# An adaLN attention + FFN layer on one core: a rebuilt prologue (load order, paired tiles, projections one group further ahead, gates on VectorE, early flag)

## Chip, cores, metric

One core of a Trainium2 chip. The metric is the device time of one execution in microseconds, the median of several. The profile's span is some 2 us shorter than the time of the same run. A run is called fast, unless it is more than 1.5% above the fastest run of the same kernel (slow); comparisons below are between fast runs where there are enough of them. "Cold" below means that TensorE runs at half of its clock, as the profile's granted clock shows it (0.50); up to a trace's first recorded change it shows 1.00 even where matmuls take twice as long (380 ns from 24.37 to 28.45 in the profile before, 190 from there).

## The reference

A transformer layer with adaptive layer norm, 2048 tokens of width 448, bf16. Attention is local: a query sees 8 keys, 2 apart, at or before its own position.

```python
mod = (silu(c) @ w_mod).reshape(1, 6, 1, 448)       # sa, ca, ga, sb, cb, gb
h = layernorm(x) * (1 + ca) + sa
x = x + ga * attention(h, wqkv, wo)                  # 16 heads of 28, window 8, dilation 2
h = layernorm(x) * (1 + cb) + sb
x = x + gb * (silu(h @ w1) @ w2)                     # 448 -> 1792 -> 448
```

## The kernel before

Tokens are split by parity, 8 tiles of 128 for each. Six groups (three for each parity) go through: projection to q, k, v; logits of blocks of 114 queries against 128 keys; exponential; multiplication by a band mask; attention output; output projection and residual; second norm; FFN. The order of instructions on each engine is the order in which the Python emits them. `weave` mixes two lists of units by their estimated cost. The gates `ga` and `gb` are multiplied into `wo` and `w2` once.

```python
    def modulate(ps, n, dst, c0, which):             # (x - mean) * rstd, transposed in PSUM -> h1T or h2T
        for k in range(KT):
            V.tensor_scalar(out=dst[:, k, c0:c0 + n], in0=ps[0:KP, k, 0:n], scalar1=..., scalar2=..., op0=ALU.mult, op1=ALU.add)

    def mod_cols(vecs, dst0):                        # modulation vectors as columns
        for i, v in enumerate(vecs):
            for j in range(KT):
                for k in range(KT):
                    T.matmul(ps[:, i, j:j + 1], lhsT=wmod[:, k, v * D + KP * j:v * D + KP * j + 128], rhs=scT[:, k:k + 1], ...)
    ...
    ps0 = transposes(normalize([0, 1, 2, 3], ...))
    mod_cols((0, 1), 0)
    modulate(ps0, 512, h1T[0], HALO, 0)
    for kk in range(KT):                             # q/k weights padded from 28 to 32 columns a head
        V.tensor_copy(out=wp[:, kk, :, 0:DH], in_=wqkv[:, kk, 0:2 * D]...)
    run(project(0))
    ln1([4, 5, 6, 7])
    mod_cols((3, 4), 2); gate(0, 2); gate(1, 5)
    G.tensor_tensor(out=wo[:], in0=wo[:], in1=gbc[0:KP, 0, :]..., op=ALU.mult)
    for f in range(NF):
        G.tensor_tensor(out=w2[:, f, :], in0=w2[:, f, :], in1=gbc[:, 1, :], op=ALU.mult)

    for k in range(NG):
        fill = []
        if k >= 1: fill += ln2_units(k - 1)          # normalise, then transposes + modulate
        if k in (0, 1): fill += project(k + 1)
        if k >= 2: fill += f2_units(k - 2)
        run(weave(l_units(k), fill))
        main = f1_units(k - 1) if k >= 1 else []
        if 2 <= k < NG - 1: main = weave(main[:-2], project(k + 1)) + main[-2:]
        if k == 0: main = [ln1 of tiles 8-11, ln1 of tiles 12-15]
        run(weave(main, o_units(k) + [ln2_stats(k)]))
    run(weave(f2_units(NG - 2), ln2_units(NG - 1))); run(f1_units(NG - 1)); run(f2_units(NG - 1))
    # here: are all softmax sums in range? count, matmul, flag, values_load -> If(bad): run a safe version
```

Of the kernel before, what the change touches and what calls it, by code (L numbers as in the profile page):

```python
# [15 lines left out]
D = 448  # L16
# [50 lines left out]
def layer(ctx, tc, io, safe):  # L67
# [17 lines left out]
    cT = ct([KP, KT], "cT")  # L85
# [13 lines left out]
    nc.scalar.dma_start(out=cT[:], in_=c.rearrange("o (k p) -> p (o k)", p=KP))  # L99
    xload(0, 4)  # L100
    nc.sync.dma_start(out=wmod[:, :, 0:2 * D], in_=rows(w_mod[:, 0:2 * D]))
    nc.sync.dma_start(out=wqkv[:, 0:2, :], in_=rows(A_wqkv)[:, 0:2, :])
    nc.sync.dma_start(out=wqkv[:, 2:4, :], in_=rows(A_wqkv)[:, 2:4, :])
    xload(4, 8)
    nc.sync.dma_start(out=wmod[:, :, 2 * D:6 * D], in_=rows(w_mod[:, 2 * D:6 * D]))
    nc.sync.dma_start(out=wo[:], in_=rows(A_wo))
# [10 lines left out]
    NV, NP, NX = 8, 5, 6  # L117
# [68 lines left out]
    def transposes(ts):  # L186
        ps = big.tile([128, KT, 512], BF16, name="ps_t", tag="big")
        for j, t in enumerate(ts):
            for k in range(KT):
                T.transpose(ps[:, k, 128 * j:128 * j + 128], t[:, KP * k:KP * k + 128], ident[:])  # L190
        return ps

    def modulate(ps, n, dst, c0, which):

        for k in range(KT):
            V.tensor_scalar(out=dst[:, k, c0:c0 + n], in0=ps[0:KP, k, 0:n], scalar1=modc[:, 2 * which + 1, k:k + 1],  # L196
                            scalar2=modc[:, 2 * which, k:k + 1], op0=ALU.mult, op1=ALU.add)

    def mod_cols(vecs, dst0):

        ps = one.tile([128, 2, KT], F32, name="ps_m", tag="one")
        for i, v in enumerate(vecs):
            for j in range(KT):
                for k in range(KT):
                    T.matmul(ps[:, i, j:j + 1], lhsT=wmod[:, k, v * D + KP * j:v * D + KP * j + 128], rhs=scT[:, k:k + 1],
                             start=(k == 0), stop=(k == KT - 1))
# [101 lines left out]
    def o_units(k):  # L308
# [34 lines left out]
        units = []  # L343
        done = list(tiles)
        for i, b in enumerate(blocks):
            units.append((500.0, lambda b=b: av(b)))
            if i:
                units.append((250.0, lambda b=blocks[i - 1]: tr(b)))
            while done and i and 128 * (done[0] + 1) <= BQ * blocks[i - 1] + nq_of(blocks[i - 1]):
                units.append((750.0, lambda a=done.pop(0): wo_unit(a)))  # L350
        units.append((250.0, lambda b=blocks[-1]: tr(b)))
        for a in done:
            units.append((750.0, lambda a=a: wo_unit(a)))
# [12 lines left out]
    def ln2_units(k):  # L366
# [5 lines left out]
        def tr():  # L372
            ps = transposes(ln2[k])
            modulate(ps, 128 * len(us), h2T[k % 2], 0, 1)
# [35 lines left out]


    def ln1(us):
        mv, rs = stats(us)
        ps = transposes(normalize(us, mv, rs))
        modulate(ps, 128 * len(us), h1T[us[0] // 8], HALO + 128 * (us[0] % 8), 0)

    mv0, rs0 = stats([0, 1, 2, 3])
    S.activation(out=scT[:], in_=cT[:], func=ACTF.Silu)
    xn0 = normalize([0, 1, 2, 3], mv0, rs0)
    ps0 = transposes(xn0)  # L420
    mod_cols((0, 1), 0)
    modulate(ps0, 512, h1T[0], HALO, 0)
# [4 lines left out]
    run(project(0))  # L427
    ln1([4, 5, 6, 7])
    mod_cols((3, 4), 2)
    gate(0, 2)  # L430
    gate(1, 5)

    def gates_apply():
        G.tensor_tensor(out=wo[:], in0=wo[:], in1=gbc[0:KP, 0, :].unsqueeze(1).to_broadcast([KP, KT, D]), op=ALU.mult)
        for f in range(NF):
            G.tensor_tensor(out=w2[:, f, :], in0=w2[:, f, :], in1=gbc[:, 1, :], op=ALU.mult)  # L436

    gates_apply()

    NG = len(GROUPS)  # L440
    for k in range(NG):
        fill = []
        if k >= 1:
            fill += ln2_units(k - 1)
        if k in (0, 1):
            fill += project(k + 1)
        if k >= 2:
# [81 lines left out]
```

## Time and profile before

| | before |
|---|---|
| time, median of 3 | 276.86 us (275.07 to 279.4) |
| span of the profiled run | 271.9 us |
| TensorE busy, mean granted clock | 201.5 us, 0.885 |
| VectorE, ScalarE, GpSimd busy | 134.3, 96.1, 34.1 us |
| first q/k matmul | 24.4 us |
| first logits of group 0 / of group 1 | 45.0 / 99.4 us |
| first FFN matmul / first of the second FFN product | 113.1 / 131.0 us |
| last output row / end of the span | 264.4 / 271.9 us |

The table is read as stages: the times are when TensorE first does the named work, and the difference of two is the length of a stage. The lines of the profile stand in the prediction.

### The profile page before, as it was taken

How to read it: one execution, taken by the hardware profiler on the slowest of the kernel's cores; microseconds unless marked ns; L12 is line 12 of the kernel's file. 1: busy time of each engine (PE TensorE's matmuls, PEld its weight loads, DVE VectorE, ACT ScalarE, POOL GpSimd, SP SyncE). 2: the span in 40 equal slices, each digit the busy share in tenths (PEclk: the TensorE clock that was granted, in tenths of full speed). 3: DMA queues.
4: the chain of work that ended last, by engine and by line, in shares of the span. 5: the costliest groups of instructions: out<-in, count | busy, mean ns of one | idle time of the engine just before them, and what ended most of it. 6: DMA issues, size and time to landing. Idle time of an engine off the chain costs nothing.

```text
span 271.9 us, 4115 instructions
## 1 busy us (share of the span) xinstructions
PE 201.5 (74%) x1738; PEld 119.6 (44%) x1738; DVE 134.3 (49%) x277; ACT 96.1 (35%) x122; POOL 34.1 (13%) x66
## 2 busy tenths in 40 slices
PE   0304959808157246979999999998999999899980
PEld 0301444403053215645455554575657654555830
DVE  1505362695574664555643616656656544543020
ACT  2000224612200012843553268731883373540500
POOL 1510016990100101000000010000100010010000
PEclk9999985656855556999999999999999999999996
DMA  5999920000000000000010000000000001000000
GB/s 139 261 281 295 292 68 1 2 0 0 0 0 2 0 0 0 2 0 2 0 54 0 0 2 17 23 14 2 0 19 17 2 0 36 17 0 29 24 17 28
DMA packets 9048, 11.22 MB, mean 41 GB/s; under 512 B 896, under 2 KB 7680, under 8 KB 9024
## 3 DMA queue, kind: packets, MB, share of 16 engines
q1 hardware_dynamic: 8560, 10.90, 14.5%
q8 instruction: 15, 0.25, 0.4%
q10 hardware_dynamic: 464, 0.00, 0.1%
q14 instruction: 9, 0.07, 0.1%
HBM read 9.06 MB, written 1.84 MB: 40 GB/s over the span
## 4 chain that ended last, share of the span: by engine, by line
PE 62%; DVE 20%; DMA 7%; ACT 3%; issue 2%; POOL 2%; SPq 1%; ACTq 0%; POOLq 0%
PE ps_y L401 16%; PE ps_h L385 14%; PE ps_qk L225 12%; DMA wmod<-in_w_mod_dram 7%; PE ps_wo L340 6%; DVE p L292 5%; PE ps_v L233 4%; PE ps_t L190 4%; DVE st L171 4%; PE ps_l L255 3%; DVE h1T L196 2%; DVE o L325 2%; ACT p L257 2%; POOL rs L174 2%; PE ps_o L320 2%
## 5 line engine op out<-in xcount | busy, mean ns | idle before, releaser
L385 PE MATMUL ps_h<-h2T,w 112*128 112x384 bf16 (+1 forms) x336 | 53.1, 308 | 0.0
L257 ACT ACTIVATE p<-ps_l 128x912 bf16<-128x912 f32 (+1 forms) x36 | 33.0, 932 | 52.3 <-PE ps_l L255 52.2
L386 ACT ACTIVATE hid<-ps_h 128x768 bf16<-128x768 f32 (+1 forms) x42 | 31.0, 740 | 48.5 <-PE ps_h L385 48.5
L401 PE MATMUL ps_y<-w,hid 128*128 128x448 bf16 x224 | 46.6, 353 | 0.0
L225 PE MATMUL ps_qk<-h1T,wp 112*128 112x456 bf16 (+2 forms) x192 | 37.8, 351 | 11.2 <-DVE qk L227 8.3
L292 DVE TENSOR_TENSOR p<-p,maskb 128x1824 bf16<-128x1824 bf16 (+1 forms) x18 | 30.1, 1673 | 28.2 <-ACT p L257 28.1
L385 PEld LDWEIGHTS <-w 112*128 112x128 bf16 x336 | 32.3, 98 | 16.4
L190 PE MATMUL ps_t<-ident,xn 128*128 128x128 bf16 x128 | 13.0, 274 | 30.5 <-DVE xn L182 30.5
L225 PEld LDWEIGHTS <-wp 112*128 112x128 bf16 x192 | 19.7, 108 | 23.9 <-issue 10.9
L401 PEld LDWEIGHTS <-hid 128*128 128x128 bf16 x224 | 20.2, 98 | 17.7
L173 POOL TENSOR_TENSOR rs<-mv,epsb 128x4 f32<-128x4 f32 (+2 forms) x10 | 2.0, 197 | 200.8 <-DVE mv L172 200.8
L190 PEld LDWEIGHTS <-xn 128*128 128x128 bf16 x128 | 10.5, 124 | 33.5 <-DVE xn L182 32.6
L340 PE MATMUL ps_wo<-wo,oT 112*128 112x448 bf16 x64 | 17.1, 396 | 8.3 <-DVE oT L334 8.3
L171 DVE BATCH_NORM_STATS2 st<-x_all 128x6 f32<-128x448 bf16 x32 | 19.3, 602 | 4.9 <-DMA x_all<-in_A_x_dram 4.9
L227 ACT CAST qk<-ps_qk 128x912 bf16<-128x912 f32 (+2 forms) x12 | 8.7, 729 | 35.6 <-PE ps_qk L225 35.5
L341 DVE TENSOR_TENSOR x_all<-ps_wo,x_all 128x448 bf16<-128x448 f32 x16 | 10.0, 625 | 19.3 <-PE ps_wo L340 19.3
L405 DVE TENSOR_TENSOR ot<-ps_y,x_all 128x448 bf16<-128x448 f32 x16 | 9.9, 621 | 18.1 <-PE ps_y L401 18.1
L182 DVE TENSOR_SCALAR xn<-x_all,mv,rs 128x448 bf16<-128x448 bf16 x32 | 11.1, 404 | 12.8 <-POOL rs L174 12.8
L227 DVE CAST qk<-ps_qk 128x912 bf16<-128x912 f32 (+2 forms) x12 | 10.4, 866 | 12.1 <-PE ps_qk L225 11.9
L233 PE MATMUL ps_v<-wqkv,h1T 112*128 112x448 bf16 x72 | 15.8, 363 | 0.7 <-ACT v L235 0.7
L196 DVE TENSOR_SCALAR h2T<-ps_t,modc 112x384 bf16<-112x384 bf16 (+1 forms) x24 | 9.3, 449 | 11.2 <-PE ps_t L190 11.2
L436 POOL TENSOR_TENSOR w<-w,gbc 128x448 bf16<-128x448 bf16 x14 | 14.8, 1100 | 0.0
(58 smaller groups left out, 157.9 us busy)
## 6 DMA issues: line engine op xcount, KB each, us to landing
w<-in_B_w_dram SPq DMA_DIRECT2D x2, 1568.0 KB, 19.0
x_all<-in_A_x_dram SPq DMA_DIRECT2D x4, 448.0 KB, 14.1
out_dram<-ot SPq DMA_DIRECT2D x16, 112.0 KB, 1.7
wmod<-in_w_mod_dram SPq DMA_DIRECT2D x1, 1568.0 KB, 17.7
wqkv<-in_A_wqkv_dram SPq DMA_DIRECT2D x2, 588.0 KB, 10.7
wmod<-in_w_mod_dram SPq DMA_DIRECT2D x1, 784.0 KB, 8.1
wo<-in_A_wo_dram SPq DMA_DIRECT2D x1, 392.0 KB, 18.3
cT<-in_c_dram ACTq DMA_DIRECT2D x1, 0.9 KB, 5.5
```

What stands on the lines that cost most here:

```text
L171: V.bn_stats(out=st[:, j, :], in_=x_all[:, u, :])
L190: T.transpose(ps[:, k, 128 * j:128 * j + 128], t[:, KP * k:KP * k + 128], ident[:])
L225: T.matmul(ps[:, j, 0:n], lhsT=wp[:, k, 16 * typ + 4 * g:16 * typ + 4 * g + 4, :].rearrange("p h d -> p (h d)"), rhs=h1T[par][:, k, HALO + ...
L227: (S.copy if on_act else V.tensor_copy)(out=dst, in_=ps[:, :, 0:n])
L233: T.matmul(ps[:, j, 0:D], lhsT=h1T[par][:, k, BQ * b + 2:BQ * b + 130], rhs=wqkv[:, k, 2 * D:3 * D], start=(k == 0), stop=(k == KT - 1))
L257: S.activation(out=pbuf(par, b)[:, t, :, :, 0:nq], in_=ps[:, :, 0:4 * nq].rearrange("p j (g q) -> p j g q", q=nq), func=ACTF.Exp, scale=SCALE)
L292: V.tensor_tensor(out=p, in0=p, in1=maskb[:, 1 if b == 0 else 0, 0:nq].unsqueeze(1).to_broadcast([128, H, nq]), op=ALU.mult)
L340: T.matmul(ps[:, 0:D], lhsT=oT[par][:, kk, 128 * a:128 * a + 128], rhs=wo[:, kk, :], start=(kk == 0), stop=(kk == KT - 1))
L385: T.matmul(ps[:, j, 0:n], lhsT=w1[:, kk, 128 * f:128 * f + 128], rhs=h2T[k % 2][:, kk, 0:n], start=(kk == 0), stop=(kk == KT - 1))
L386: S.activation(out=hid[k % 2][:, 2 * i:2 * i + 2, 0:n], in_=ps[:, :, 0:n], func=ACTF.Silu)
L401: T.matmul(ps[:, 0:D], lhsT=hid[k % 2][:, f, 128 * j:128 * j + 128], rhs=w2[:, f, :], start=(f == 0), stop=(f == NF - 1))
L436: G.tensor_tensor(out=w2[:, f, :], in0=w2[:, f, :], in1=gbc[:, 1, :], op=ALU.mult)
```

## The change

Its intent: get TensorE going earlier, and keep it fed until the dense part.

```diff
-    nc.sync.dma_start(out=wqkv[:, 0:2, :], ...)           # q, k and v columns together
+    xload(0, 2); xload(2, 4)                              # was xload(0, 4)
+    nc.sync.dma_start(out=wqkv[:, 0:2, 0:2 * D], ...)     # q and k first, v later; wo before the rest of w_mod
@@ mod_cols
+                    m = 128 if j < KT - 1 else KP
-                    T.matmul(ps[:, i, j:j + 1], lhsT=wmod[:, k, v*D + KP*j : v*D + KP*j + 128], ...)
+                    T.matmul(ps[0:m, i, j:j + 1], lhsT=wmod[:, k, v*D + KP*j : v*D + KP*j + m], ...)
@@ modulate
+            if k in act: S.activation(out=o, in_=i, func=ACTF.Identity, scale=scale, bias=shift)    # act=(1, 3) in the first norm
@@ gates
-        G.tensor_tensor(wo) and 14 x G.tensor_tensor(w2[:, f, :])
+        V.tensor_tensor(wo)                               # with late_mod, at the end of group 0's logits
+        V.tensor_tensor(w2[:, f0:f1, :])                  # (0, 7) and (7, 14), at the end of group 1's logits
@@ main order
-    run(project(0)); ln1([4, 5, 6, 7])
+    run(weave(project(0), ln1_units([4, 5, 6, 7])))
     for k in range(NG):
+        if k == 0:   fill = project(1) + [late_mod]
+        elif k == 1: fill = ln2_units(0) + project(3) + [gate_w2(0, 7), gate_w2(7, 14)]
+        else:
+            f2 = f2_units(k - 2)
+            fill = f2[:2] + ln2_units(k - 1) + f2[2:]     # was ln2_units first
+        main for k == 0: project(2) + ln1 of 8-11 + ln1 of 12-15;  for 2 <= k < NG - 2: project(k + 2) with f1
+    # output projections one block later; ln2_stats ahead of the last two f1 units
+    bad = check_sums()                                    # before the last second product, was at the very end
```

(Cut: the conditioning vector `c` is loaded in rows and transposed by a small matmul instead of a strided load, ten v buffers instead of eight, the first two logits units of group 1 ahead of its `fill`, helper signatures.)

More of the change, by code (lines that the diff above doesn't have):

```diff
@@ L84, in layer @@
     x_all = ct([128, 16, D], "x_all")
-    cT = ct([KP, KT], "cT")
+    c4 = ct([KT, KP], "c4")
+    sc4 = ct([KT, KP], "sc4")
     wmod = ct([KP, KT, 6 * D], "wmod")
@@ L97, in xload @@
         nc.sync.dma_start(out=x_all[:, u0:u1, :], in_=x_view[u0 // 8, u0 % 8:u0 % 8 + u1 - u0].rearrange("a p d -> p a d"))
-    nc.scalar.dma_start(out=cT[:], in_=c.rearrange("o (k p) -> p (o k)", p=KP))
-    xload(0, 4)
+    nc.scalar.dma_start(out=c4[:], in_=c.rearrange("o (k p) -> (o k) p", p=KP))
+    xload(0, 2)
+    xload(2, 4)
     nc.sync.dma_start(out=wmod[:, :, 0:2 * D], in_=rows(w_mod[:, 0:2 * D]))
-    nc.sync.dma_start(out=wqkv[:, 0:2, :], in_=rows(A_wqkv)[:, 0:2, :])
-    nc.sync.dma_start(out=wqkv[:, 2:4, :], in_=rows(A_wqkv)[:, 2:4, :])
+    nc.sync.dma_start(out=wqkv[:, 0:2, 0:2 * D], in_=rows(A_wqkv[:, 0:2 * D])[:, 0:2, :])
+    nc.sync.dma_start(out=wqkv[:, 2:4, 0:2 * D], in_=rows(A_wqkv[:, 0:2 * D])[:, 2:4, :])
     xload(4, 8)
+    nc.sync.dma_start(out=wqkv[:, :, 2 * D:3 * D], in_=rows(A_wqkv[:, 2 * D:3 * D]))
+    nc.sync.dma_start(out=wo[:], in_=rows(A_wo))
     nc.sync.dma_start(out=wmod[:, :, 2 * D:6 * D], in_=rows(w_mod[:, 2 * D:6 * D]))
-    nc.sync.dma_start(out=wo[:], in_=rows(A_wo))
     xload(8, 12)
@@ L116, in layer @@
     hid = [ct([128, NF, 384], f"hid{i}") for i in range(2)]
-    NV, NP, NX = 8, 5, 6
+    NV, NP, NX = 10, 5, 6
     vb = [ct([128, H, 32], f"v{i}") for i in range(NV)]
@@ L184, in normalize, with transposes, modulate @@
         return got
-    def transposes(ts):
-        ps = big.tile([128, KT, 512], BF16, name="ps_t", tag="big")
+    def transposes(ts, ps=None, j0=0):
+        if ps is None:
+            ps = big.tile([128, KT, 512], BF16, name="ps_t", tag="big")
         for j, t in enumerate(ts):
+            c0 = 128 * (j0 + j)
             for k in range(KT):
-                T.transpose(ps[:, k, 128 * j:128 * j + 128], t[:, KP * k:KP * k + 128], ident[:])
+                T.transpose(ps[:, k, c0:c0 + 128], t[:, KP * k:KP * k + 128], ident[:])
         return ps
-    def modulate(ps, n, dst, c0, which):
+    def modulate(ps, p0, n, dst, c0, which, act=()):
         for k in range(KT):
-            V.tensor_scalar(out=dst[:, k, c0:c0 + n], in0=ps[0:KP, k, 0:n], scalar1=modc[:, 2 * which + 1, k:k + 1],
-                            scalar2=modc[:, 2 * which, k:k + 1], op0=ALU.mult, op1=ALU.add)
+            o, i = dst[:, k, c0:c0 + n], ps[0:KP, k, p0:p0 + n]
+            scale, shift = modc[:, 2 * which + 1, k:k + 1], modc[:, 2 * which, k:k + 1]
+            if k in act:
+                S.activation(out=o, in_=i, func=ACTF.Identity, scale=scale, bias=shift)
+            else:
+                V.tensor_scalar(out=o, in0=i, scalar1=scale, scalar2=shift, op0=ALU.mult, op1=ALU.add)
     def mod_cols(vecs, dst0):
@@ L204, in mod_cols @@
                 for k in range(KT):
-                    T.matmul(ps[:, i, j:j + 1], lhsT=wmod[:, k, v * D + KP * j:v * D + KP * j + 128], rhs=scT[:, k:k + 1],
+                    m = 128 if j < KT - 1 else KP
+                    T.matmul(ps[0:m, i, j:j + 1], lhsT=wmod[:, k, v * D + KP * j:v * D + KP * j + m], rhs=scT[:, k:k + 1],
                              start=(k == 0), stop=(k == KT - 1))
@@ L341, in wo_unit @@
             V.tensor_tensor(out=x_all[:, u, :], in0=ps[:, 0:D], in1=x_all[:, u, :], op=ALU.add)
-        units = []
-        done = list(tiles)
-        for i, b in enumerate(blocks):
-            units.append((500.0, lambda b=b: av(b)))
-            if i:
-                units.append((250.0, lambda b=blocks[i - 1]: tr(b)))
-            while done and i and 128 * (done[0] + 1) <= BQ * blocks[i - 1] + nq_of(blocks[i - 1]):
-                units.append((750.0, lambda a=done.pop(0): wo_unit(a)))
-        units.append((250.0, lambda b=blocks[-1]: tr(b)))
-        for a in done:
-            units.append((750.0, lambda a=a: wo_unit(a)))
+        units, waiting, done = [], list(tiles), 0
+        for i in range(len(blocks) + 2):
+            if i < len(blocks):
+                units.append((500.0, lambda b=blocks[i]: av(b)))
+            if 1 <= i <= len(blocks):
+                units.append((250.0, lambda b=blocks[i - 1]: tr(b)))
+            if i >= 2:
+                done = BQ * blocks[i - 2] + nq_of(blocks[i - 2])
+                while waiting and 128 * (waiting[0] + 1) <= done:
+                    units.append((750.0, lambda a=waiting.pop(0): wo_unit(a)))
         return units
@@ L373, in tr @@
             ps = transposes(ln2[k])
-            modulate(ps, 128 * len(us), h2T[k % 2], 0, 1)
+            modulate(ps, 0, 128 * len(us), h2T[k % 2], 0, 1)
         return [(10.0, norm), (700.0, tr)]
@@ L409, in f2_units, with check_sums @@
         return units
-    def ln1(us):
-        mv, rs = stats(us)
-        ps = transposes(normalize(us, mv, rs))
-        modulate(ps, 128 * len(us), h1T[us[0] // 8], HALO + 128 * (us[0] % 8), 0)
-    mv0, rs0 = stats([0, 1, 2, 3])
-    S.activation(out=scT[:], in_=cT[:], func=ACTF.Silu)
-    xn0 = normalize([0, 1, 2, 3], mv0, rs0)
-    ps0 = transposes(xn0)
+    def check_sums():
+        n = 2 * NB * H
+        ok = small.tile([128, n], F32, name="ok", bufs=1)
+        cnt = small.tile([128, 1], F32, name="cnt", bufs=1)
+        flag = small.tile([1, 1], I32, name="flag", bufs=1)
+        rcf = rc[:].rearrange("p b h -> p (b h)")
+        V.tensor_scalar(out=ok[:], in0=rcf, scalar1=LO, scalar2=None, op0=ALU.is_ge)
+        V.scalar_tensor_tensor(out=ok[:], in0=rcf, scalar=HI, in1=ok[:], op0=ALU.is_le, op1=ALU.mult)
+        V.tensor_reduce(out=cnt[:], in_=ok[:], axis=AX.X, op=ALU.add)
+        ps = one.tile([128, 512], F32, name="ps_f", tag="one")
+        T.matmul(ps[0:1, 0:1], lhsT=cnt[:], rhs=onesf[:], start=True, stop=True)
+        V.tensor_scalar(out=flag[:], in0=ps[0:1, 0:1], scalar1=-1.0, scalar2=float(128 * n), op0=ALU.mult, op1=ALU.add)
+        return nc.values_load(flag[:], min_val=0, max_val=128 * n)
@@ new lines, in ln1_units, with st, norm, tr @@
+    def ln1_units(us):
+        held = {}
+        def st():
+            held["s"] = stats(us)
+        def norm():
+            mv, rs = held["s"]
+            held["x"] = []
+            for j, u in enumerate(us):
+                t = xn[xc[0] % NX]
+                xc[0] += 1
+                V.tensor_scalar(out=t[:, 0:D], in0=x_all[:, u, :], scalar1=mv[:, j, 0:1], scalar2=rs[:, j:j + 1], op0=ALU.subtract, op1=ALU.mult)
+                held["x"].append(t)
+        def tr():
+            ps = transposes(held["x"])
+            modulate(ps, 0, 128 * len(us), h1T[us[0] // 8], HALO + 128 * (us[0] % 8), 0, act=(1, 3))
+        return [(10.0, st), (10.0, norm), (900.0, tr)]
@@ L421, in layer @@
+    st0 = stats([0, 1])
+    st1 = stats([2, 3])
+    S.activation(out=sc4[:], in_=c4[:], func=ACTF.Silu)
+    ps_c = one.tile([128, 512], F32, name="ps_c", tag="one")
+    T.matmul(ps_c[0:KP, 0:KT], lhsT=sc4[:], rhs=ident[0:KT, 0:KT], start=True, stop=True)
+    S.copy(out=scT[:], in_=ps_c[0:KP, 0:KT])
+    xa = normalize([0, 1], *st0)
+    ps0 = transposes(xa)
+    xb = normalize([2, 3], *st1)
     mod_cols((0, 1), 0)
-    modulate(ps0, 512, h1T[0], HALO, 0)
+    ps1 = transposes(xb)
+    modulate(ps0, 0, 256, h1T[0], HALO, 0, act=(1, 3))
@@ L423, in layer @@
+    modulate(ps1, 0, 256, h1T[0], HALO + 256, 0, act=(1, 3))
     for kk in range(KT):
@@ L426, in layer @@
     V.tensor_copy(out=screp[:], in_=scT[:].unsqueeze(2).to_broadcast([KP, KT, 128]))
-    run(project(0))
-    ln1([4, 5, 6, 7])
-    mod_cols((3, 4), 2)
-    gate(0, 2)
-    gate(1, 5)
-    def gates_apply():
-        G.tensor_tensor(out=wo[:], in0=wo[:], in1=gbc[0:KP, 0, :].unsqueeze(1).to_broadcast([KP, KT, D]), op=ALU.mult)
-        for f in range(NF):
-            G.tensor_tensor(out=w2[:, f, :], in0=w2[:, f, :], in1=gbc[:, 1, :], op=ALU.mult)
-    gates_apply()
+    run(weave(project(0), ln1_units([4, 5, 6, 7])))
@@ L440, in layer, with late_mod, gate_w2 @@
+    def late_mod():
+        mod_cols((3, 4), 2)
+        gate(0, 2)
+        gate(1, 5)
+        V.tensor_tensor(out=wo[:], in0=wo[:], in1=gbc[0:KP, 0, :].unsqueeze(1).to_broadcast([KP, KT, D]), op=ALU.mult)
+    def gate_w2(f0, f1):
+        V.tensor_tensor(out=w2[:, f0:f1, :], in0=w2[:, f0:f1, :], in1=gbc[:, 1, :].unsqueeze(1).to_broadcast([128, f1 - f0, D]), op=ALU.mult)
     NG = len(GROUPS)
     for k in range(NG):
-        fill = []
-        if k >= 1:
-            fill += ln2_units(k - 1)
@@ L445, in layer @@
-        if k in (0, 1):
-            fill += project(k + 1)
-        if k >= 2:
-            fill += f2_units(k - 2)
-        run(weave(l_units(k), fill))
-        main = []
-        if k >= 1:
-            main = f1_units(k - 1)
-        if 2 <= k < NG - 1:
-            main = weave(main[:-2], project(k + 1)) + main[-2:]
-        if k == 0:
-            main = [(1000.0, lambda: ln1([8, 9, 10, 11])), (1000.0, lambda: ln1([12, 13, 14, 15]))]
-        run(weave(main, o_units(k) + [(2500.0, lambda k=k: ln2_stats(k))]))
+        if k == 0:
+            fill = project(1) + [(2000.0, late_mod)]
+        elif k == 1:
+            fill = ln2_units(0) + project(3) + [(10.0, lambda: gate_w2(0, 7)), (10.0, lambda: gate_w2(7, 14))]
+        else:
+            f2 = f2_units(k - 2)
+            fill = f2[:2] + ln2_units(k - 1) + f2[2:]
@@ new lines, in layer @@
+        lu = l_units(k)
+        n0 = 2 if k == 1 else 0
+        run(lu[:n0] + weave(lu[n0:], fill))
+        if k == 0:
+            main = project(2) + ln1_units([8, 9, 10, 11]) + ln1_units([12, 13, 14, 15])
+        else:
+            main = f1_units(k - 1)
+            if 2 <= k < NG - 2:
+                main = weave(main[:-2], project(k + 2)) + main[-2:]
+        run(weave(main[:-2], o_units(k)) + [(0.0, lambda k=k: ln2_stats(k))] + main[-2:])
+    if not safe:
+        bad = check_sums()
@@ L460, in layer @@
     run(f2_units(NG - 1))
-    if safe:
-        return None
-    ok = small.tile([128, 2 * NB * H], F32, name="ok", bufs=1)
-    cnt = small.tile([128, 1], F32, name="cnt", bufs=1)
-    flag = small.tile([1, 1], I32, name="flag", bufs=1)
-    rcf = rc[:].rearrange("p b h -> p (b h)")
-    V.tensor_scalar(out=ok[:], in0=rcf, scalar1=LO, scalar2=None, op0=ALU.is_ge)
-    V.scalar_tensor_tensor(out=ok[:], in0=rcf, scalar=HI, in1=ok[:], op0=ALU.is_le, op1=ALU.mult)
-    V.tensor_reduce(out=cnt[:], in_=ok[:], axis=AX.X, op=ALU.add)
-    ps = one.tile([128, 512], F32, name="ps_f", tag="one")
-    T.matmul(ps[0:1, 0:1], lhsT=cnt[:], rhs=onesf[:], start=True, stop=True)
-    V.tensor_scalar(out=flag[:], in0=ps[0:1, 0:1], scalar1=-1.0, scalar2=float(128 * 2 * NB * H), op0=ALU.mult, op1=ALU.add)
-    return nc.values_load(flag[:], min_val=0, max_val=128 * 2 * NB * H)
+    return None if safe else bad
 @with_exitstack
```

## The prediction

> **What bounds the kernel now.** I read the slices of the page first (busy tenths, 6.8 us each), then the timeline of the first 130 us, then sums by stretch, then the end of the chain of waits.
>
> ```profile
> PE   0304959808157246979999999998999999899980
> ...
> POOL 1510016990100101000000010000100010010000
> PEclk9999985656855556999999999999999999999996
> ...
> GB/s 139 261 281 295 292 68 1 2 0 0 0 0 2 0 0 0 2 0 2 0 54 0 0 2 17 23 14 2 0 19 17 2 0 36 17 0 29 24 17 28
> ```
>
> From slice 17 on (113 us) TensorE is busy at 90% or more at full clock: it is the bound there. Before that it is idle or at about half clock. The slices read as two kernels: a ragged prologue of some 110 us and a dense part of some 150 us. By stretch (columns: span, then busy us and count of PE, PEld, DVE, ACT, POOL, then granted clock):
>
> ```profile
> 53.50:61.60 8.10, 0.00 (x0) 0.00 (x0) 8.10 (x3) 1.69 (x2) 8.10 (x8) 0.63 0.01 2
> ...
> 131.00:163.00 32.00, 31.51 (x239) 17.25 (x237) 13.57 (x25) 15.04 (x19) 0.89 (x2) 1.00 0.04 12
> 163.00:194.00 31.00, 29.34 (x296) 18.21 (x295) 18.58 (x37) 16.33 (x22) 1.04 (x2) 1.00 0.04 12
> ```
>
> The timeline (start, us, engine, line, what; in brackets the idle time before it and what ended it) says why the prologue is slow, in three places. The first three lines are TensorE's alone:
>
> ```profile
> 12.87 0.93 PE L205 MATMUL ps_m<-scT,wmod 112*128 112x1 bf16 x28
> 21.54 0.26 PE L205 MATMUL ps_m<-scT,wmod 112*128 112x1 bf16 x4 [7.74 <-DMA wmod<-in_w_mod_dram]
> 24.37 8.29 PE L225 MATMUL ps_qk<-h1T,wp 112*128 112x456 bf16 x32 [2.56 <-DVE wp L424]
> ...
> 47.00 14.76 POOL L436 TENSOR_TENSOR w<-w,gbc 128x448 bf16<-128x448 bf16 x14
> ...
> 49.63 11.24 DVE L292 TENSOR_TENSOR p<-p,maskb 128x1824 bf16<-128x1824 bf16 x1 [7.07 <-ACT p L257]
> ...
> 74.00 1.01 POOL L174 TENSOR_TENSOR rs<-rs,negh 128x4 f32<-128x4 f32 x1
> 75.04 1.31 DVE L182 TENSOR_SCALAR xn<-x_all,mv,rs 128x448 bf16<-128x448 bf16 x4 [1.40 <-POOL rs L174]
> ```
>
> First, 28 of the 32 modulation matmuls run at 12.9 us, the last four only at 21.5, after a load. They are the last column block of the second vector: columns 784 to 912 of w_mod, 16 columns past the first load's 896, so they wait for the second w_mod load, though its 16 columns are never used. Second, the mask multiply at 49.63 takes 11.24 us, against a median of 1.11 us, while GpSimd gates w2. Third, from 70 to 104 us VectorE runs norm statistics and attention output in one queue, itself waiting 1.40 us for GpSimd's power step in each round, and TensorE waits behind it.
>
> [...] the 456-column matmuls from 24.37 go at 380 ns until 28.45, then at 190. [...]
>
> **The change, part by part.**
>
> *Start.* The last block of each vector is now 112 columns wide, so the false wait goes. q and k weights load before v weights. Landing times of the old loads fit "bytes ahead of it divided by the GB/s row, plus 1.5 us". With 0.459 MB of tokens, 0.803 of w_mod and 0.803 of q/k weights ahead, that gives 9.6 us for w_mod, 12.6 for q/k, and 14.3 for the next four token tiles (2.52 MB). Chain: first pair of tiles lands at about 5.2; four statistics at 0.73 end at 8.2; normalised 8.95 and 10.15; 32 matmuls at about 0.033 end near 11; the second pair's transposes near 12; modulation in halves over VectorE and ScalarE until 12.8; first weight copy 0.32. First q/k matmul at about 13.1 against 24.4: **-11.3**.
>
> *First projections with tiles 4 to 7.* The build order puts their transposes after only 8 of the 32 q/k matmuls. Those end at 16.2 (8 x 0.38, cold). Statistics cannot start before 14.3: 2.9, GpSimd 1.3, the first normalise 0.4, so TensorE idles until 19.2. Then transposes 1.9, 24 q/k matmuls (3.0 cold, 1.6, 1.6), 16 v matmuls 3.2: first logits near 30.7, against 45.0. Cumulative **-14.3**; the new wait at 16 eats part of the overlap.
>
> *Logits of group 0.* GpSimd gates no more. VectorE does it: wo 1.1 us, w2 in two operations of 1.9 (rate of the mask, 1824 elements in 1.11 us). ScalarE now paces: 8 exponentials 7.5, table load 1.3, two q/k copies 1.5, three v copies 1.5, two gate copies 1.1, plus the first matmuls and the last mask: about 15.3 against 24.6 (45.0 to 69.6). It ends at 46. Cumulative **-24**.
>
> *Tiles 8 to 15 with attention output of group 0.* VectorE has 8+3 statistics at 0.73, 8 normalises at 0.33, four modulations at 0.54 (the other four go to ScalarE), four attention blocks (0.87+0.39), three residual adds at 0.62, two q/k copies at 0.63: 21.0 us. Statistics are still behind attention in its order, each round holds a GpSimd step of 1.3 us, and TensorE sits between them at half clock, so I add about 8 us of waits: 46 to 75, against 69.6 to 99.4. Cumulative **-24.5**. This stage also takes in group 2's projection.
>
> *Logits of group 1.* This holds group 3's projection (32 matmuls at 190 and 16 at 190 ns warm, 9.2 us), the second layer norm and the w2 gating: about 18 us, starting cold, against 13.7. Cumulative **-20**. The first FFN stays at 16 to 17.
>
> *Dense part.* The 9.2 us of group 3's projection is gone from it and TensorE bounds it, so all of that counts: **-29**. FFN matmuls ahead of the transposes, and output projections one block later, fill waits: TensorE idles only about 3.4 us of 131 to 264 (133 less the 129.6 busy in the stretches), so I give 2: **-31**.
>
> *End.* The old end, from the chain of waits:
>
> ```profile
> 263.80 0.62 DVE ot L405
> 264.42 0.23 DVE ok L469
> ...
> 265.90 0.15 DVE flag L474
> ```
>
> The check takes 1.6 us behind the last output, then 5.85 us pass to the span's end (271.9) with the flag's register load, the branch and the barrier. Now the flag is read before the last FFN. [...] At the end remain an output store (1.7 us to landing), branch and barrier. About 4 saved[...]: **-34** as the rounded sum.
>
> 276.9 - 34 is 243; I put **242 us**.
>
> **Rivals.**
>
> 1. *The start moves and the prologue stretches by as much*, because VectorE's queue from 70 to 100 us is the real bound. For it: 19.7 us of VectorE work there do not shrink much and gating adds 4.9. Against: the 11.2 us mask stall is real idle time on TensorE (0.00 busy in 53.5 to 61.6), and projections now fill gaps. It would keep only the mask and the dense part's gain: about 255.
>
> 2. *TensorE falls to half clock from 20 to 90 us.* The group-0 logits then cost TensorE about 23 us, not 15, and group 1's projection 6 more: about 254. The clock row (5 and 6 in most of the prologue) speaks for it; work packed more densely after 20 us speaks against.
>
> 3. *It goes better*: half of the 8 us of waits do not come and everything is warm after 25 us. Then 232 or so; TensorE's 201.5 us of busy time, inflated by cold matmuls, would allow even less.
>
> 4. *Loads land later*, since q/k rows are shorter (1792 bytes, not 2688). Tiles and w_mod rows are that short already and ran at 260 to 295 GB/s, so I expect under 2 us.
>
> **Range and chances.** The -11.3, the mask and the dense part rest on single lines and together are over 28 us. What is uncertain is how the two prologue stages fill: 12 us either way. Range 230 to 256. To stay within 2% (271.3) nearly all of it would have to come back. Faster 0.97, same 0.02, slower 0.01.
>
> **What would show each step.** The 32 modulation matmuls in one run near 10 to 11 us; first q/k matmul at 12 to 14.5; a TensorE gap of about 3 us before tiles 4 to 7 are transposed; every mask multiply at about 1.1 us, GpSimd busy below 20 us in all; logits of group 0 over by 44 to 50; first FFN matmul at 88 to 98; from its end to the last output about 11 us less than 131 to 264; [...] under 4 us after the last output. I am wrong if the first q/k matmul stays past 16 us, if the gating on VectorE holds up attention output by more than its 4.9 us, or if the dense stages show new waits for ScalarE.

Passages are cut out of it where the text is marked: rules and figures that no trace or run of this case shows. That GpSimd's gating makes the mask slow thus rests on the two lines of the trace alone, the one mask of 11.24 us beside 14.76 us of gating, against a median of 1.11 us; it was the author's reading until the gating was moved alone, below. Terms are cut from the sum: its parts came to -34 us with a term for TensorE's stall at the flag, which took a little over 1 us back and whose size no trace showed. The terms left add up to -35; the figure stays 242 us.

## The result

| | before | after | after / before |
|---|---|---|---|
| time, median of 4 | 277.1 us (275.07 to 279.4) | 245.38 us (243.57 to 251.07) | 0.8855 (0.8753 to 0.8957) |
| span of the profiled run | 271.9 | 244.5 | |

The ratio is the mean time of one kernel's fast runs over that of the other's of the same rounds, so not quite the ratio of the medians. The output is correct. The three fast runs after are 246.31, 244.46 and 243.57 us, at granted clocks of 0.929, 0.949 and 0.950; the profile is that of the first.

Stages, in us. "Predicted" is what the working of the prediction gives for the same points.

| TensorE first does | before | predicted | after |
|---|---|---|---|
| q/k matmul | 24.4 | 13.1 | 15.3 |
| logits, group 0 | 45.0 | 30.7 | 31.8 |
| logits, group 1 | 99.4 | 75 | 73.7 |
| FFN | 113.1 | 93 | 92.6 |
| second FFN product | 131.0 | 109.5 | 108.9 |
| (dense part, to the last output row) | 133.4 long | 11 less | 131.4 long |
| (from there to the end of the span) | 7.5 long | 4 less | 4.2 long |

First the slices of the page after the change (6.1 us each):

```profile
PE   0555979982522997899999959899599999989992
...
POOL 3801000001030000010000100000100010010000
PEclk9998999998555699999999988999889999999999
```

GpSimd's long 9s are gone, TensorE is dense from slice 13 (80 us) instead of 17 (113 us). But in the dense part there are two new 5s, with the clock at 8 around them. They were not there before. The timeline of the prologue after the change shows the modulation matmuls in one run, and the masks without the long wait:

```profile
10.10 1.55 PE L215 MATMUL ps_m<-scT,wmod 112*128 112x1 bf16 x32 [2.01 <-DMA wmod<-in_w_mod_dram]
...
15.32 3.22 PE L235 MATMUL ps_qk<-h1T,wp 112*128 112x456 bf16 x8 [2.80 <-DVE wp L471]
...
36.58 1.11 DVE L302 TENSOR_TENSOR p<-p,maskb 128x1824 bf16<-128x1824 bf16 x1 [6.62 <-ACT p L267]
```

The dense part by stretch, before and after (span, then busy us and count of TensorE, weight loads, VectorE, ScalarE, GpSimd, then clock):

```profile
131.04:264.42 133.38, 129.38 (x1108) 77.45 (x1104) 63.82 (x127) 63.83 (x80) 3.88 (x8) 1.00 0.04 14
```

```profile
108.91:240.34 131.43, 123.63 (x1074) 75.36 (x1070) 64.03 (x132) 61.41 (x75) 5.10 (x10) 0.97 0.05 14
```

TensorE's idle time there grew from 4.0 to 7.8 us, and its busy time fell by 5.75 us only, though the 9.2 us of group 3's projection were gone. The rest, about 3.5 us, is what cold matmuls took longer (clock 0.97 instead of 1.00). The clock is at half twice there (columns: span, then TensorE's busy us and count, clock, DMA):

```profile
144.91:148.32 3.41, 3.41 (x17) 0.50 0.10 34
175.62:179.03 3.41, 3.41 (x24) 0.50 0.02 5
```

The timeline at the first of the two 5s, VectorE and TensorE:

```profile
141.61 1.11 DVE L302 TENSOR_TENSOR p<-p,maskb 128x1824 bf16<-128x1824 bf16 x1 [6.46 <-ACT p L267]
142.64 0.70 DVE L185 TENSOR_SCALAR xn<-x_all,mv,rs 128x448 bf16<-128x448 bf16 x2
...
143.09 0.70 PE L195 MATMUL ps_t<-ident,xn 128*128 128x128 bf16 x8 [2.81 <-DVE xn L185]
```

TensorE waits 2.81 us for the normalised rows (`xn`) of the second norm. The normalise itself waits for nothing but its place: it stands behind the first mask multiply in VectorE's queue, and the mask waits for two exponentials, which wait for ScalarE's switch of function tables (`ACT_TABLE_LOAD`, 1.28 us) behind the last SiLUs. At 175.57 it happens again, 2.60 us. This is what `f2[:2]` ahead of the norm did. In stages with three or four blocks of logits, `weave` emits the second logits unit, which ends with the mask, before it gets past the two FFN pieces to the normalise. In stages 2 and 5, with two blocks, the normalise comes first and there is no gap.

At the end, the flag and the last output row:

```profile
219.01 0.15 DVE L433 TENSOR_SCALAR flag<-ps_f 1x1 int32<-1x1 f32 x1 [0.74 <-PE ps_f L432]
219.71 1.11 PE L411 MATMUL ps_y<-w,hid 128*128 128x448 bf16 x5 [0.74 <-DVE flag L433]
...
239.72 0.62 DVE L415 TENSOR_TENSOR ot<-ps_y,x_all 128x448 bf16<-128x448 f32 x1 [2.02 <-PE ps_y L411]
```

TensorE pays 0.74 us in the middle. 4.2 us remain after the last row (240.34 to 244.5), against 7.5.

### The profile page after: what moved, and what is told of

The parts are those of the page before. It is cut to its first block, busy times and chain, and to the rows that moved or that the text cites. A ratio compares the mean times of both kernels' runs of the same rounds, so it can differ in the third digit from the quotient of the medians.

```text
span 244.5 us, 4117 instructions
## 1 busy us (share of the span) xinstructions
PE 196.3 (80%) x1739; PEld 118.7 (49%) x1739; DVE 125.3 (51%) x274; ACT 102.9 (42%) x133; POOL 16.8 (7%) x55
## 4 chain that ended last, share of the span: by engine, by line
PE 67%; DVE 15%; ACT 8%; DMA 3%; issue 3%; POOL 1%; SPq 0%; ACTq 0%
PE ps_h L395 18%; PE ps_y L411 17%; PE ps_qk L235 10%; PE ps_v L243 5%; PE ps_wo L350 5%; PE ps_t L195 4%; ACT p L267 4%; DMA wmod<-in_w_mod_dram 3%; PE ps_l L265 3%; DVE st L174 3%; DVE p L302 2%; DVE o L335 2%; PE ps_o L330 2%; ACT h1T L204 2%; ACT L267 2%
## 5 line engine op out<-in xcount | busy, mean ns | idle before, releaser
L411 PE MATMUL ps_y<-w,hid 128*128 128x448 bf16 x224 | 48.5, 365 | 0.7 <-DVE flag L433 0.7
L302 DVE TENSOR_TENSOR p<-p,maskb 128x1824 bf16<-128x1824 bf16 (+1 forms) x18 | 19.9, 1107 | 37.5 <-ACT p L267 37.5
L235 PE MATMUL ps_qk<-h1T,wp 112*128 112x456 bf16 (+2 forms) x192 | 35.3, 334 | 4.2 <-DVE wp L471 2.8
L195 PE MATMUL ps_t<-ident,xn 128*128 128x128 bf16 x128 | 13.3, 276 | 26.4 <-DVE xn L449 14.7
L235 PEld LDWEIGHTS <-wp 112*128 112x128 bf16 x192 | 18.6, 103 | 15.6 <-issue 5.2
L174 DVE BATCH_NORM_STATS2 st<-x_all 128x6 f32<-128x448 bf16 x32 | 19.2, 601 | 2.4 <-DMA x_all<-in_A_x_dram 2.4
L204 ACT ACTIVATE h1T<-ps_t,modc 112x512 bf16<-112x512 bf16 (+1 forms) x10 | 6.8, 691 | 31.3 <-DVE h1T L206 31.3
L176 POOL TENSOR_TENSOR rs<-mv,epsb 128x2 f32<-128x2 f32 (+2 forms) x11 | 2.3, 206 | 199.8 <-DVE mv L175 199.8
L245 ACT CAST v<-ps_v 128x448 bf16<-128x448 f32 x18 | 8.8, 536 | 16.4 <-PE ps_v L243 16.3
L265 PE MATMUL ps_l<-qk 28*128 28x114 bf16 (+1 forms) x288 | 13.8, 221 | 2.3 <-ACT h1T L204 2.3
L350 PE MATMUL ps_wo<-wo,oT 112*128 112x448 bf16 x64 | 15.5, 367 | 0.2
L265 PEld LDWEIGHTS <-qk 28*128 28x128 bf16 x288 | 8.0, 97 | 13.7 <-issue 13.3
```

The costliest lines, as they stand in the source:

```text
L174: V.bn_stats(out=st[:, j, :], in_=x_all[:, u, :])
L195: T.transpose(ps[:, k, c0:c0 + 128], t[:, KP * k:KP * k + 128], ident[:])
L204: S.activation(out=o, in_=i, func=ACTF.Identity, scale=scale, bias=shift)
L235: T.matmul(ps[:, j, 0:n], lhsT=wp[:, k, 16 * typ + 4 * g:16 * typ + 4 * g + 4, :].rearrange("p h d -> p (h d)"), rhs=h1T[par][:, k, HALO + ...
L265: T.matmul(ps[:, j, g * nq:(g + 1) * nq], lhsT=qk[par][r:r + DH, 4 + g, BQ * b + 2:BQ * b + 130], rhs=qk[par][r:r + DH, g, HALO + BQ * b:H ...
L302: V.tensor_tensor(out=p, in0=p, in1=maskb[:, 1 if b == 0 else 0, 0:nq].unsqueeze(1).to_broadcast([128, H, nq]), op=ALU.mult)
```

## The experiments

Twelve kernels ran, all with a correct result. Each call had its own runs of the kernel before and ran on another chip, so kernels of different calls are compared by their ratio to it.

### The small edits one at a time, in the kernel before

Runs of before: median 275.79 us, mean of the fast ones 275.7.

**Only the 112-column block.**

```diff
+                    m = 128 if j < KT - 1 else KP
-   lhsT=wmod[..., v * D + KP * j:v * D + KP * j + 128]
+   lhsT=wmod[..., v * D + KP * j:v * D + KP * j + m]
```

> The kernel before with one edit: the last column block of each modulation vector is 112 columns wide, so that it no longer reads 16 columns of the second w_mod load. My theory: the false wait is worth the whole move of the start. The four late matmuls follow the other 28 at 13.9 us, modulation ends near 16.2, the first q/k matmul comes at about 16.5 instead of 24.4, everything behind it moves along: -8 us, time near 269 (ratio 0.971). Rival: what follows is bound by something else (VectorE's queue, GpSimd's gating, later loads), so most is lost again before 100 us: less than 3 us, ratio above 0.99.

Measured: 267.94 us, ratio 0.9708 (0.9649 to 0.9767). First q/k matmul at 17.25, last output row at 258.95 instead of 264.4. The theory's ratio was 0.971. One false dependence on 16 unused columns is a quarter of the whole change (7.9 of 31.7 us by the medians), and what follows takes back little: in the traces 5.5 of the 7.1 us of the start remain at the last row, and the profile of before is that of a fast run (273.64 us). The rival falls.

**Only the gating on VectorE.**

```diff
-   G.tensor_tensor(wo); for f in range(NF): G.tensor_tensor(w2[:, f, :])
+   V.tensor_tensor(wo); for f in (0, 7): V.tensor_tensor(w2[:, f:f + 7, :])
```

> The kernel before with one edit: wo and w2 are gated on VectorE (one and two operations) at the same place, GpSimd does none of it. Theory: the mask multiply of 11.24 us at 49.6 falls to 1.11; the gating costs VectorE 1.1 + 2 x 1.9 us, of which most lies before the first mask anyway; -9 to -10 us, time near 267 (ratio 0.965). Rival: VectorE is the bound there, so the 4.9 us show in full and only 5 us or less are left (ratio 0.98 or more).

Measured: 267.76 us median. Only one of the four runs is fast (263.37); the others, 267.5 to 268.5, lie over 1.5% above it, so there is no interval. Median against median it is -8.0, the one fast run against the mean of before -12.3. The trace (of a slow run) shows the mechanism: the first mask takes 1.11 us instead of 11.24, group 1's logits begin at 89.8 instead of 99.4. The rival (5 us or less) falls; the size is settled only to 8 to 12 us.

**Only the flag earlier.**

```diff
+   bad = check of the sums, values_load             # ahead of the last second product
    run(weave(f2_units(NG - 2), ln2_units(NG - 1))); run(f1_units(NG - 1)); run(f2_units(NG - 1))
-   check of the sums, values_load
```

> The kernel before with one edit: the check of the softmax sums and the read of its flag stand before the last FFN. Theory from the two traces: the time from the last output row to the span's end falls from 7.5 to about 4.2 us, TensorE pays a gap of about 0.7 us: -2.5 us, ratio 0.991. Rival: the register load stalls several engines in the middle, and nothing is left: ratio 0.998 or more.

Measured: 273.19 us, ratio 0.9898 (0.9842 to 0.9955), -2.8 us by the means of fast runs. From the last row to the end of the span 4.0 us instead of 7.5. As the theory had it.

**All three.**

> The kernel before with all three small edits (112 columns, gating on VectorE, flag early). Theory: they act in different places and add up, -8 -9.5 -2.5 = -20 us, time near 257 (ratio 0.928); the rest of the whole change's -31.7 us, about 12, would then belong to the reordering (loads, pairs, weaving, projections ahead). Rival: they overlap, the earlier start only lengthens the later wait for VectorE: less than 15 us (ratio 0.946 or more).

Measured: 261.3 us median of 254.84, 259.93, 262.67 and 263.6. Again only one run is fast, and no interval. The fast one is 20.8 us below before, which is the theory's sum; the median is only 14.5 below, which is the rival's side. Inconclusive on whether they add up in full. If the fast run is taken, the reordering is worth about 10 us of the change (254.8 to 244.8, the mean of the changed kernel's fast runs, in another call). Of its parts, the load order, the paired tiles and the weaving of tiles 4 to 7 were never run alone.

### What the dense part lost, and the split of the modulation

Four kernels. Before: median 274.82 us, but five of its eleven runs are slow, and the record gives the verdict "unclear" for all four kernels, though their intervals lie far below 0.98. Among themselves they are compared by the means of their fast runs.

**The changed kernel again.**

> The changed kernel itself once more, beside the three variants of it in this call: ratio 0.8855 before, so 0.875 to 0.896; the two TensorE gaps of 2.8 and 2.6 us ahead of the second-norm transposes of stages 3 and 4 show again, as they follow from the order of VectorE's queue.

Measured: 245.28 us, ratio 0.8933 (0.8872 to 0.8993). The gaps are there again, 2.81 us at 142.6 and 2.60 at 173.5.

**The normalise ahead of the FFN pieces.**

```diff
-            fill = f2[:2] + ln2_units(k - 1) + f2[2:]
+            ln = ln2_units(k - 1)
+            fill = ln[:1] + f2[:2] + ln[1:] + f2[2:]
```

> The changed kernel with the second norm's normalise emitted ahead of the first FFN pieces (so ahead of the first mask in VectorE's queue), the transposes staying where they are. Theory: the changed kernel lost most of what the dense part gained (2 us instead of 11) to two gaps, 2.8 and 2.6 us, in which the transposes wait for a normalise queued behind a mask multiply, which waits for the exponentials, the table load and the last SiLUs; behind each gap TensorE runs cold for some us (about 3.5 us in all). Then the gaps go and 5.4 to 9 us are gained: time near 238 (ratio to before 0.860). Rival: the transposes are not what holds TensorE, the next matmul waits for ScalarE's exponentials as well, and less than 2 us come of it.

Measured: 239.09 us (237.81 to 239.69, all six fast), ratio 0.8724 (0.8686 to 0.8761): 5.7 us less than the repeat by the means of the fast runs (6.2 by the medians). The theory's 5.4 to 9 holds at its lower end, and the rival falls. The same place in its timeline:

```profile
136.71 0.70 DVE L185 TENSOR_SCALAR xn<-x_all,mv,rs 128x448 bf16<-128x448 bf16 x2 [1.08 <-POOL rs L177]
...
140.68 0.62 PE L195 MATMUL ps_t<-ident,xn 128*128 128x128 bf16 x8
...
142.09 1.11 DVE L302 TENSOR_TENSOR p<-p,maskb 128x1824 bf16<-128x1824 bf16 x1 [4.67 <-ACT p L267]
```

The normalise runs before the mask, the transposes follow without a wait. And the dense part by stretch:

```profile
109.39:232.08 122.69, 120.30 (x1074) 74.21 (x1070) 63.74 (x132) 61.30 (x75) 5.10 (x10) 1.00 0.05 15
```

With the same 1074 matmuls, TensorE's busy time falls from 123.63 to 120.30, so the cold matmuls are gone as well, and its idle time from 7.8 to 2.4. The dense part is 10.7 us shorter than before the change: what the prediction had promised (11), and the changed kernel had not delivered.

**All first-norm modulation on VectorE.** In the changed kernel half of it is on ScalarE. Its timeline shows the two engines taking turns:

```profile
11.94 0.41 DVE L206 TENSOR_SCALAR h1T<-ps_t,modc 112x256 bf16<-112x256 bf16 x1
12.45 0.56 ACT L204 ACTIVATE h1T<-ps_t,modc 112x256 bf16<-112x256 bf16 x1 [8.96 <-DVE h1T L206]
13.05 0.73 DVE L206 TENSOR_SCALAR h1T<-ps_t,modc 112x256 bf16<-112x256 bf16 x2 [0.70 <-ACT h1T L204]
13.50 1.02 ACT L204 ACTIVATE h1T<-ps_t,modc 112x256 bf16<-112x256 bf16 x2 [0.48 <-DVE h1T L206]
```

```diff
-    modulate(..., act=(1, 3))
+    modulate(...)
```

> The changed kernel with all first-norm modulation on VectorE instead of half on ScalarE. In the changed kernel's trace the two engines take turns (each ScalarE piece waits for the VectorE piece before it and the other way round), so the split buys nothing. Theory: the start stays within 0.5 us (8 pieces of about 0.37 on VectorE against 3.6 us of taking turns), and the exponentials of group 1 come 2 us earlier because ScalarE does not sit in the modulation of tiles 12 to 15: -1.5 to -2.5 us against the changed kernel. Rival: the split does help, as VectorE is the bound between 45 and 75 us: +1 to +3 us.

Measured: 247.5 us, ratio 0.9043 (0.899 to 0.9095): 2.5 us slower by the means of the fast runs, against the theory. Yet its trace is 0.5 us ahead of the repeat of the changed kernel at the first second-product matmul (107.98 against 108.44), and loses afterwards. The dense part, in the repeat and then here:

```profile
108.44:238.41 129.97, 122.17 (x1074) 74.54 (x1070) 63.97 (x132) 61.45 (x75) 5.11 (x10) 0.99 0.05 15
```

```profile
107.98:239.40 131.42, 123.62 (x1074) 75.37 (x1070) 64.04 (x132) 61.42 (x75) 5.10 (x10) 0.97 0.05 15
```

The idle time is the same, 7.80 us. The 1.45 us between them are busy time of the same 1074 matmuls: the repeat has half clock once (175.28 to 178.69), this kernel twice, and the changed kernel's own first profile (131.43 us) twice as well. So this loss in the dense part is not work of the edit; it can come and go with one and the same program. The fast runs here have clocks of 0.916 to 0.936, those of the repeat 0.929 to 0.949; why they are lower in all of them is not shown. The suspicion fell on the gaps and not on the modulation; see the same edit without gaps below.

**Four tiles for the modulated activations.**

```diff
-    h1T = [ct([KP, KT, CW], f"h1T{p}") for p in range(2)]
+    h1T = [[ct([KP, CW], f"h1T{p}_{k}") for k in range(KT)] for p in range(2)]
```

> The changed kernel with the modulated activations kept in four tiles, one for each block of 112 features, and nothing else changed. Theory: the taking of turns comes from the order kept between writers of one tile; with four tiles the ScalarE and VectorE pieces run side by side, first q/k matmul near 14.0 instead of 15.3, and 1 us less before the exponentials of group 1: -2 to -2.5 us. Rival: the turns come from the shared PSUM tile that both read; then they still alternate and nothing changes.

Measured: 246.17 us, ratio 0.8971 (0.8904 to 0.9039): no difference clear of noise. The timeline still alternates:

```profile
12.01 0.56 ACT L205 ACTIVATE h1T<-ps_t,modc 112x256 bf16<-112x256 bf16 x1 [8.53 <-DVE h1T L207]
12.61 0.73 DVE L207 TENSOR_SCALAR h1T<-ps_t,modc 112x256 bf16<-112x256 bf16 x2 [0.70 <-ACT h1T L205]
```

My theory falls, the rival stands: separate output tiles change nothing. By elimination the order comes from the PSUM tile that both read (they also share the small tile `modc` of scales and shifts, which was not tested apart). VectorE's k = 2 at 12.61 reads other columns of it than ScalarE's k = 1, and still waits 0.70 us for that one. Whether two smaller PSUM tiles would let the engines run side by side was not tried.

### Projections, modulation without gaps, and a better version

Four kernels. Before: median 273.49 us. All build on the kernel with the normalise moved (ratio 0.8724 above).

**Projections back by one group.**

```diff
-            fill = ln2_units(0) + project(3) + ...
+            fill = ln2_units(0) + project(2) + ...
-            main = project(2) + ln1 ...;   if 2 <= k < NG - 2: ... project(k + 2)
+            main = ln1 ...;                if 2 <= k < NG - 1: ... project(k + 1)
```

> a_norm (the changed kernel with the second normalise ahead of the first FFN pieces) with the projections put back one group, as in the kernel before. Theory: projections one group ahead pay because they fill TensorE in a stretch where VectorE holds it back (45 to 75 us), while in the dense part each costs its full time: taking them back adds 9 us to the dense part, removes 4 to 5 from the group-1 logits and about 1 from the stretch of tiles 8 to 15: +3 to +5 us against a_norm, ratio 0.884 to 0.892. Rival: it is only moved work, 0 within 1 us.

Measured: 247.65 us, ratio 0.8994 (0.8936 to 0.9051), 7 to 9 us more (ratios 0.8724 and 0.8994 of 273.5, or the medians). The sign is right, the size twice what I expected. By the milestones: the dense part is 131.1 us instead of 122.7 (+8.4), group 1's logits 16.2 instead of 19.0. The stretch from group 0's to group 1's logits does not get shorter without group 2's projection, 44.3 us instead of 41.9; its clock is 0.69 instead of 0.83. And the first FFN takes 19.3 us instead of 16.3, at a clock of 0.91 instead of 1.00. So the projection in that stretch was free: it filled idle time (14.6 us are idle with it, 17.7 without), and in this trace TensorE is colder without it.

**Modulation on VectorE, now without gaps.**

> a_norm with all first-norm modulation on VectorE. a_modV came out slower than the changed kernel (0.9043 against 0.8933), although its trace is 0.5 us ahead at the first second-FFN matmul: it lost in the dense part. Theory: what it lost there was the clock, at the two gaps that a_norm has not; then here it is 0 to 1.5 us faster than a_norm, ratio 0.867 to 0.873. Rival: modulation on VectorE is itself dearer, +1 us or more, ratio above 0.876.

Measured: 236.23 us, ratio 0.8648 (0.8601 to 0.8694), 2 to 3 us faster; the two intervals just overlap. The same edit that cost 2.5 us with the gaps gains about that much without them. This supports the reading that its loss was clock, not work; it does not prove it run by run. In the traces the dense part is the same (122.7 us), and 1.5 us of the gain lie in group 1's logits, 17.5 us instead of 19.0.

**Statistics of tiles 8 to 15 early, transposes of tiles 4 to 7 one unit later.**

```diff
-    run(weave(project(0), ln1_units([4, 5, 6, 7])))
+    pr, ln = project(0), ln1_units([4, 5, 6, 7])
+    run(pr[:1] + ln[:2] + pr[1:2] + ln[2:] + pr[2:])
+    l8, l12 = ln1_units([8, 9, 10, 11]), ln1_units([12, 13, 14, 15])
+    run(l8[:1] + l12[:1])
...
-            main = project(2) + ln1_units([8, 9, 10, 11]) + ln1_units([12, 13, 14, 15])
+            main = project(2) + l8[1:] + l12[1:]
```

> a_norm with the statistics of tiles 8 to 15 moved ahead of the logits of group 0, where VectorE is idle for 6.6 us, and the transposes of tiles 4 to 7 behind two q/k units instead of one. Theory: the stretch from 45 to 75 us is bound by VectorE's queue; with 5.9 us taken out of it the TensorE gaps of 5.5 and 6.5 us ahead of the transposes of tiles 8 to 15 shrink by 4 and 3, the one of 2.8 us at 18.5 goes: -6 to -9 us against a_norm, near 231 (ratio 0.84 to 0.85). Rival: TensorE's half clock and ScalarE set that stretch, and the statistics now delay the masks of group 0: within 2 us.

Measured: 226.66 us, ratio 0.8283 (0.8239 to 0.8327), 12 us less, more than expected. TensorE's transposes of tiles 8 to 15, in the changed kernel and then here:

```profile
61.98 1.89 PE L195 MATMUL ps_t<-ident,xn 128*128 128x128 bf16 x16 [5.45 <-DVE xn L449]
71.83 1.89 PE L195 MATMUL ps_t<-ident,xn 128*128 128x128 bf16 x16 [6.47 <-DVE xn L449]
```

```profile
53.97 1.32 PE L195 MATMUL ps_t<-ident,xn 128*128 128x128 bf16 x16 [1.03 <-DVE xn L449]
60.34 1.89 PE L195 MATMUL ps_t<-ident,xn 128*128 128x128 bf16 x16 [4.29 <-DVE xn L449]
```

The two waits fall from 11.9 to 5.3 us. From group 0's to group 1's first logits it is 34.0 us instead of 41.9, at a clock of 0.96 instead of 0.83. The other 4 us come before: first logits at 28.2 instead of 32.2, by the later transposes (the wait there falls from 2.75 to 1.06 us, and the 16 transposes behind it take 1.31 us instead of 1.89). VectorE's queue was the bound of this stretch. Of the 7.9 us gained in it, 6.6 are TensorE's idle time (14.6 to 8.0) and 1.3 its busy time, as less of it runs at half clock.

**The best version: the last two together, and w2 gated earlier.**

```diff
-            fill = ln2_units(0) + project(3) + [gate_w2(0, 7), gate_w2(7, 14)]
+            fill = ln2_units(0) + [gate_w2(0, 7), gate_w2(7, 14)] + project(3)
```

> a_stats with all modulation on VectorE and the two w2 gating operations moved ahead of group 3's projection, where VectorE is idle for 4.5 us, instead of ahead of the attention output of group 1. Theory: the attention output of group 1 starts 3.4 us earlier, TensorE's waits in the first FFN shrink by 1 to 2 us, modulation gives up to 1: -1.5 to -3 us against a_stats, near 229. Rival: no difference, as TensorE has the FFN to do meanwhile.

Measured: 222.08 us (220.79 to 224.87), ratio 0.8102 (0.8057 to 0.8146). It beats the kernel before by 19% and the changed kernel by 23 us. That is 4.6 to 5 us less than the version above, more than the 1.5 to 3 expected. Against it: group 1's logits 17.7 instead of 19.4 us, the first FFN 13.8 instead of 16.3; TensorE is busy in all of the latter (13.83 of 13.83 us). The gating that stood in front of attention output in VectorE's queue did cost TensorE 2 us: modulation on VectorE alone, in the experiment before the last, had left the first FFN at 16.3.

## Why the prediction was right, and where it was not

The time, 245.4, lies within 230 to 256 and 3.4 us above the 242 predicted. In spans the change gave 27.4 us (271.9 to 244.5), in medians 31.7, because the profiled run of before was among the faster ones (273.64 us) and that of after was the slowest of its fast ones. That the number came so close is partly luck: the steps add up spans, and there 27.4 of the promised 34 us came, with one step failed by 9. Point by point:

- **Start, "-11.3": mechanism right, mis-sized, -9.1 measured** (-10.2 in the repeat, 14.18). The false wait went, and alone it gave 8 us. At 15.3 the first q/k matmul came later than the prediction's own sign (12 to 14.5), though before its limit of 16. The term too small was the modulation "in halves over VectorE and ScalarE until 12.8": the engines took turns on the shared PSUM tile (waits of 0.48 to 0.77 us from piece to piece) and were done at 15.6, 3.6 us after the first piece (VectorE alone, in the run for it, took 2.64 for all eight); and the 32 modulation matmuls took 1.55 us, not 1.0.
- **Projection of group 0 with tiles 4 to 7, cumulative "-14.3": -13.3.** The predicted new wait is there, 2.76 us at 18.5.
- **Logits of group 0 and the stretch to group 1, cumulative "-24.5": -25.7.** GpSimd's gating was the cause of the long mask: with the gating on VectorE every mask takes 1.1 us, in every kernel here that has it (means of 1.10 to 1.11 us). The 8 us of added waits were about right: VectorE is idle for 6.8 of the 26.6 us from the last mask to group 1's logits.
- **Group 1's logits and first FFN, cumulative "-20": -20.5 at the first FFN matmul, -22.1 at its end.**
- **Dense part, "9.2 + 2": this step failed; -2.0 measured.** "FFN matmuls ahead of the transposes [...] fill waits" was wrong: they pushed the normalise behind the mask in VectorE's queue and made two gaps, 2.8 and 2.6 us, with two stretches of half clock behind them that cost about 3.5 us. With the normalise alone moved back, the dense part gives 10.7. I had read the order on TensorE and not followed the same units on VectorE. The last sign of error named in the prediction, new waits for ScalarE in the dense stages, is close to how it showed: VectorE's mask waited for ScalarE, and TensorE for VectorE behind it.
- **End, "about 4 saved": 3.3 saved, and 0.74 paid in the middle**; alone, in the kernel before, 2.8 in all. What the prediction set against it for the flag was more than the 0.74 us measured; from the flag's end (219.16) to the next matmul it is 0.55 us. The time after the last output also missed its sign (under 4 us; 4.2).

Some sums and readings in the working are slightly off, with no effect on the result: the terms for tiles 4 to 7 end at 18.9, not 19.2; the four stretches hold 129.4 us of TensorE work, not 129.6; the second rival adds up to 256, not 254; and the old page's slices are not all 9s from 113 us on (a 7 and three 8s follow).

Of the rivals, none came true in full. The first was right that VectorE bounds the stretch before group 1; moving statistics out of it gave 8 us there.

## What to carry to other kernels

Follow a reordering on every engine's queue: a unit placed early for TensorE can be late for VectorE, and a cheap operation behind one that waits is as late as that one (0.70 us of normalising behind a mask that waited 6.46). Look for waits on bytes that are never used (7.74 us here), above all where a slice is rounded up across the edge of a load. Work moved into idle time of the bound engine can be free: taking group 2's projection out of such a stretch did not shorten it (44.3 against 41.9 us). Before explaining a small loss, compare idle and busy time of the same matmuls: a loss in busy time alone was clock here (1.45 us, with the same 7.80 us idle).

## What else the traces show

- Half clock behind short gaps. After the change, gaps of 2.81 and 2.60 us (they end at 143.09 and 175.57) were followed by half clock from 144.91 to 148.32 us, about 2 us after the first gap had ended, and from 175.62 to 179.03. Ten matmuls of 448 columns took 3.50 us in the first, 350 ns each, against 195 in the kernel before (28 in 5.46). The two falls are 30.7 us apart, nine times the 3.41 us that each lasted, and in the profiles before and after all falls lie whole multiples of 3.41 us apart (5, 5 and 57 of them before; 11, 25, 9 and 20 after). In the repeat of the changed kernel the first gap, again 2.81 us, was not followed by half clock: ten such matmuls from 144.73 took 2.06 us. What decides it was not shown.
- The long mask. It took 11.24 us (12.21 in the run with only the flag moved) against back-to-back GpSimd operations of about 1.05 us each (14 in 14.76 us): it lasted through about ten of them. Whether it stood still or ran slowly, the trace does not show.
- Two readers of one PSUM tile. ScalarE and VectorE take turns here even where they read different columns (VectorE's piece at 13.05 waits 0.70 us for ScalarE's); whether the chip needs it was not tested. Sharing the modulation bought nothing (ratio 0.8648 with all of it on VectorE against 0.8724).
